# Blocks of scores turned on VectorE: all stored by one DMA and fetched by four, and a planner that counts eight transfers under way and later landings

## The chip, the cores and the metric

The kernel runs on 1 core of one Trainium2 chip. The metric is the device time of one execution in microseconds (us); the median of the runs before is 1094.97 us.

## What is computed

Two batches of 3136 tokens go through three layers, all in float32:

```python
scores = matmul(z, z.T) / S                   # z: 2 x 3136 x 64
x = u * matmul(maximum(scores, 0) ** 2, v)    # u, v: 2 x 3136 x 256
h = maximum(x @ w_in, 0)                      # 256 -> 1024
conv = sum of conv_w[k] * h shifted by k - 1  # three taps along the tokens
x = (h * sigmoid(conv)) @ w_out               # 1024 -> 256
xn = (x - mean) / sqrt(var + 1e-6) * g_ln
out = x + maximum(xn @ w_ch1, 0) @ w_ch2
```

Since the scores are z times its own transpose, the squared score block (i, j) is the transpose of block (j, i). The kernel uses that.

## The kernel before, in words

**Tiling.** A matrix product in float32 is made of three products of halves (high*high, low*high, high*low). Each batch is cut into seven chunks of queries (4, 4, 3, 4, 3, 3, 4 tiles of 128 tokens; the last tile of a batch has 64), so there are 14 chunks. For each chunk and each of the 25 tiles j of keys, a block of squared scores "a" (128 keys x 384, 448 or 512 queries) is needed. It is split into `ah` (ACT, sometimes DVE) and `al` (DVE), and six products on PE add it to the sums `av` (lines 793, 795, 796). After a chunk, `gate_u` multiplies the sums with u on DVE (line 811), and the result goes to DRAM as `gated`. The two dense layers read that back in blocks of three token tiles (`make_x`, `mlps`); their products (`hps`, `y`, `h2ps`) stand between the products of later chunks.

**Blocks that are turned instead of computed again.** A block whose mirror image was computed in an earlier chunk of the same batch is not computed. When the earlier block was made, `spill` had it turned in 32 x 32 pieces on DVE (`bl`, line 649) and stored in DRAM. `land` (lines 689 and 697) fetches it back into one of the six places of tag "a". Two ways of storing exist:

- Most blocks are stored by one DMA into `turned` (line 657) and fetched by four DMAs of 32 partitions each, in pieces of 32 elements (line 697).
- Blocks of the (chunk, later chunk) pairs in `EARLY`, here chunks 0 and 1 of the first batch for chunks 5 and 6, are stored by four DMAs in pieces of 32 elements into `mirror` (line 664) and fetched by one DMA with long rows (line 689).

In all, 154 blocks are fetched: 138 by four DMAs and 16 by one. The centred rows of the second dense layer take a similar way for most blocks of tokens (`centred<-tn` line 1064, then four DMAs `tn<-centred`, line 1070).

**What sets the order.** Nothing of the order is written by hand. `Program.order` simulates the five engines: each operation has a price per engine, a due time (worked back from the end through what depends on it, `dues`), and places in rings of buffers that it must hold. At each step an idle engine takes the operation that is ready and due first. All DMAs are issued by SP, in the planned order; an instruction of SP that waits holds up all that stand behind it. The landing of a DMA is planned from `LANDS` (1.6), its size over `RATE`, and `LATE` by name; the fetch of a block, named "land", has no `LATE`. Where the plan leaves PE idle for more than 0.225 us, products with zeros (`fill`, line 1268) are put into PE's order, one per 0.125 us of the gap. Once planned, the order of each engine is fixed, whatever the chip does.

Of the kernel before, what the change touches and what calls it, by code (L numbers as in the profile page):

```python
# [15 lines left out]
P = 128  # L16
# [7 lines left out]
SQ = 32  # L24
# [5 lines left out]
LAG0 = 130.0  # L30
LAG1 = 6.0
LAG2 = 10
EARLY = (0, 5), (0, 6), (1, 5), (1, 6)
FETCH = ("SP",)
LAND_US = {"SP": 0.56, "ACT": 0.6}

UP1, DOWN1, TURN, UP2 = 0.4, 0.14, 0.6, 0.36
LENGTH = 14.0, 14.0, 8.0, 8.0
# [36 lines left out]

AFTER = {"PE": 0.2, "ACT": 0.165, "DVE": 0.15, "POOL": 0.13, "SP": 0.0}
RATE, LANDS = 300.0, 1.6
LATE = {"z1": 1.4, "v1": 1.6, "u": 1.0, "wi": 0.8, "wo": 0.8, "w1": 0.8, "w2": 0.8, "x in": 1.2, "lh": 0.6, "spill": 0.6}
SPILL_KB, LAND_KB = 0.53, 0.91
ENGINES = ("PE", "ACT", "DVE", "POOL", "SP")  # L80

# [9 lines left out]
class Op:  # L91
    __slots__ = (
        "ways", "fn", "before", "left", "after", "bufs", "due", "ready", "start", "end", "n", "engine", "late",
        "name", "port", "kb", "adds", "spare",
    )


class Program:
# [4 lines left out]
        self.tags = tags  # L103
        self.ops, self.writers, self.readers = [], {}, {}

    def op(self, ways, fn, reads=(), writes=(), adds=(), takes=(), due=None, late=None, name="", port=False, kb=None):


        o = Op()
        o.ways, o.fn, o.due, o.late, o.name, o.port, o.kb = ways, fn, due, late, name, port, kb  # L110
        o.before, o.after, o.n = set(), [], len(self.ops)
        o.adds, o.spare = tuple(adds), None
        for k in reads:
            assert k in self.writers, (name, k)
            o.before.update(self.writers[k])
            self.readers.setdefault(k, []).append(o)
        for k in writes:
            o.before.update(self.writers.get(k, ()))
            o.before.update(self.readers.pop(k, ()))
            self.writers[k] = [o]  # L120
        for k in adds:
            o.before.update(self.readers.get(k, ()))
            self.writers.setdefault(k, []).append(o)
        o.before.discard(o)
        bufs = []
        for k in (*reads, *writes, *adds, *((t,) for t in takes)):
            if isinstance(k[0], Buf) and k[0] not in bufs:
                bufs.append(k[0])
        for b in bufs:
            b.users.append(o)  # L130
        o.bufs = bufs
        self.ops.append(o)
        return o
# [7 lines left out]
    def dues(self):  # L141
# [6 lines left out]
        for o in reversed(self.ops):  # L148
# [7 lines left out]
            for b in o.bufs:  # L156
                if b.order is not None:
                    k = b.tag, b.order
                    wanted[k] = min(wanted.get(k, o.due), o.due)

    def order(self):
        self.dues()
        for o in self.ops:
            for b in o.bufs:
                b.left = len(b.users)
            o.ready = 0.0
        live = {t: [] for t in self.tags}
        turn = {t: 1 for t in self.tags}
# [7 lines left out]
        for o in self.ops:  # L176
            if not o.left:
                enter(o)
        done, now, port, owner, moved_at = [], 0.0, 0.0, None, 0.0
        busy = dict.fromkeys(ENGINES, 0.0)  # L180
        while len(done) < len(self.ops):
            nxt = None

            def later(t):
                nonlocal nxt
                if t > now + 1e-9 and (nxt is None or t < nxt):
                    nxt = t

            def room(o):
                want = {}  # L190
                for b in o.bufs:
                    if b.taken:
                        continue
                    if b.order is not None and b.order != turn[b.tag]:
                        return False
                    want[b.tag] = want.get(b.tag, 0) + 1
                for tag, n in want.items():
                    held = [b for b in live[tag] if b.left or b.free_at > now]
                    live[tag] = held
                    if len(held) + n > self.tags[tag][0]:  # L200
                        for b in held:
                            if not b.left:
                                later(b.free_at)
                        return False
                for b in o.bufs:
                    if not b.taken and b.kind in CAPS and sum(x.kind == b.kind for x in live[b.tag]) >= CAPS[b.kind]:
                        for x in live[b.tag]:
                            if not x.left:
                                later(x.free_at)
                        return False  # L210
                return True

            moved = False
            for e in ENGINES:
                if free[e] > now + 1e-9:
                    later(free[e])
                    continue
                best = None
                for o in open_[e]:
                    if o.ready > now + 1e-9:  # L220
                        later(o.ready)
                        continue
                    if (e == "POOL" or e == "DVE" and o.port) and port > now + 1e-9 and owner != e:
                        later(port)
                        continue
                    key = (o.ways[0][0] != e, o.due, o.n)
                    if best is not None and key >= best[0]:
                        continue
                    if key[0]:

                        x = o.ways[0][0]
                        wait = max(0.0, free[x] - now) + sum(
                            p.ways[0][1] for p in open_[x]
                            if p.ways[0][0] == x and p.ready <= now and (p.due, p.n) <= (o.due, o.n)
                        )
                        if wait < HELP * dict(o.ways)[e]:
                            continue
                    if room(o):
                        best = key, o
                if best is None:  # L240
                    continue
                o = best[1]
                us = dict(o.ways)[e]
                for x, _ in o.ways:
                    open_[x].remove(o)
                o.engine, o.start, o.end = e, now, now + self.lasts(o, e, us)
                free[e] = now + us
                if o.kb is not None:
                    moved_at = max(moved_at, now + us) + o.kb / RATE
                    o.end = moved_at + LANDS + LATE.get(o.name, 0.0)  # L250
                if e == "POOL" or e == "DVE" and o.port:
                    port, owner = now + us + 0.06, e
                busy[e] += us
                later(free[e])
                for b in o.bufs:
                    if not b.taken:
                        b.taken = True
                        live[b.tag].append(b)
                        if b.order is not None:
                            turn[b.tag] += 1  # L260
                    b.left -= 1
                    b.free_at = max(b.free_at, o.end)
                for a in o.after:
                    a.left -= 1
                    a.ready = max(a.ready, o.end if a.ways[0][0] != e or e != "PE" else free[e])
                    if not a.left:
                        enter(a)
                done.append(o)
                moved = True
            if moved:  # L270
                continue
            if nxt is None:
                stuck = sorted((o for e in ENGINES for o in open_[e]), key=lambda o: o.due)
                raise RuntimeError(f"stuck at {now}: {[(o.name, o.left, [b.tag for b in o.bufs if not b.taken]) for o in stuck[:20]]}")
            now = nxt
# [26 lines left out]
def attn_moe_kernel(ctx: ExitStack, tc: tile.TileContext, zt, ut, v, w_in, conv_w, w_out, g_ln, w1, w2, out):  # L302
# [73 lines left out]
    op = pr.op  # L376
# [32 lines left out]
        return [(e, us[e]) for e in (first, *others)]  # L409

    def dma(fn, kb, **kw):
        return op([("SP", 0.45)], lambda e: fn(), late=LANDS + kb / RATE, kb=kb, **kw)


    zp = [(o, min(o + 512, ZW)) for o in range(0, ZW, 512)]
# [181 lines left out]
    centred = [dram.tile([4, SQ, NTT * D], F32, tag=f"centred{i}", name="centred") for i in range(2)]  # L597
# [30 lines left out]
    turned = {}  # L628
# [15 lines left out]
    def spill(c, j, ab):  # L644
        w = chunks[c][1] - chunks[c][0]
        b = buf("bl")
# [3 lines left out]
            reads=[(ab, 0)], writes=[(b, 0)], name="bl", port=True,  # L650
# [14 lines left out]

        if early(c, chunk_of[j]):
            op(
                [("SP", 1.95)], write_mirrored, reads=[(b, 0)], writes=[("turned", c, j)],
                late=LANDS + LAND_KB * w / RATE, kb=LAND_KB * w, due=1e4, name="spill",
            )  # L670
            return
        op(
            [("SP", 0.4)], write, reads=[(b, 0)], writes=[("turned", c, j)],
            late=LANDS + SPILL_KB * w / RATE, kb=SPILL_KB * w, due=1e4, name="spill",
        )

# [186 lines left out]
    def mlps(c):  # L863
        when = whens[c]
        s, e_ = blocks[c]
        n = e_ - s
# [186 lines left out]
        if far:  # L1053
# [14 lines left out]
            def fetch(e):  # L1068
# [4 lines left out]
                    )  # L1073

            op(
                [("SP", 2.05)], fetch, late=LANDS + n / RATE, kb=n, reads=[("centred", c % 2)], writes=[(tn, 0)],
                name="xn in",
            )

            def landed(d):  # L1080
# [261 lines left out]
```

## Time and profile before

| | us |
|---|---|
| median of 3 runs (lowest, highest) | 1094.97 (1094.73, 1096.04) |
| the profiled execution | 1097.35 |
| its span, first to last instruction | 1095.6 |
| PE busy (matmul) / PEld (weight load) | 1084.7 / 1018.4 |
| DVE / ACT / POOL busy | 881.4 / 724.2 / 37.4 |
| DMA queue of the kernel | 47.3% of 16 engines |

The times of parts below are of the profiled execution. A matmul is recorded from its start to its modelled end, and the next one starts well before that end, so the idle time of PE is less than the time that PE lost. The weight loads (PEld), one ahead of each matmul, show the lost time more directly: a load that comes late shows idle time and what ended it. The engine names are those of the profile: PE is TensorE, DVE VectorE, ACT ScalarE, POOL GpSimd, SP SyncE (SPq where it issues DMAs). The granted clock of TensorE is 1.00 throughout.

### The profile page before, as it was taken

To read this page: it belongs to the slowest core of one execution; us is meant where nothing else is said; L and a number is where in the kernel's file an instruction comes from. 1 tells how busy PE (TensorE), PEld (TensorE's weight loads), DVE (VectorE), ACT (ScalarE), POOL (GpSimd) and SP (SyncE) were. 2 spreads that over 40 slices of the span, in tenths; PEclk is the share of its full clock that TensorE was granted. 3 is DMA by queue.
4 is the path that set the end of the run, shared out by engine and by line. 5 is a ranking of instruction groups with operands and counts; after the bars stand their busy time and mean duration, and the time that the engine had idled before them with its cause. 6 is when DMAs were issued, how large, how long until landed. Compare 5 with 4: busy or idle time off the path is not lost.

```text
span 1095.6 us, 19246 instructions
## 1 busy us (share of the span) xinstructions
PE 1084.7 (99%) x6569; PEld 1018.4 (93%) x6569; DVE 881.4 (80%) x1890; ACT 724.2 (66%) x1500; POOL 37.4 (3%) x54
## 2 busy tenths in 40 slices
PE   9999999999999999999999999999999999999998
PEld 7878888999999899999999999999999999999998
DVE  7999899899996988787868788878678585868674
ACT  7768788886765767675757666656666463646452
POOL 2100000000101000000000000000000000000000
PEclk9999999999999999999999999999999999999999
DMA  6786878677867232322243425142635557520000
GB/s 203 201 202 141 191 172 184 133 201 173 231 142 166 84 101 63 102 79 79 78 115 96 110 59 129 42 111 60 156 77 121 109 99 147 96 78 25 25 16 20
DMA packets 379106, 126.45 MB, mean 115 GB/s; under 512 B 278272, under 2 KB 368896, under 8 KB 379008
## 3 DMA queue, kind: packets, MB, share of 16 engines
q1 hardware_dynamic: 379008, 125.23, 47.3%
q8 instruction: 51, 0.84, 0.3%
q14 instruction: 47, 0.39, 0.1%
HBM read 70.25 MB, written 51.97 MB: 112 GB/s over the span
## 4 chain that ended last, share of the span: by engine, by line
PE 85%; DVE 4%; DMA 4%; ACT 3%; SPq 2%; issue 1%; DVEq 0%; POOL 0%; ACTq 0%
PE av L793 11%; PE av L796 11%; PE av L795 10%; PE y L900 8%; PE y L902 8%; PE y L901 8%; PE h2ps L884 4%; PE h2ps L886 4%; PE h2ps L885 4%; PE hps L884 4%; PE hps L885 4%; PE hps L886 4%; PE s L751 3%; PE s L752 3%; DMA land<-turned 2%
## 5 line engine op out<-in xcount | busy, mean ns | idle before, releaser
L793 PE MATMUL av<-ah,vh 128*128 128x512 f32 (+2 forms) x700 | 257.4, 368 | 3.4 <-ACT ah L401 1.7
L796 PE MATMUL av<-ah,vl 128*128 128x512 f32 (+2 forms) x700 | 256.0, 366 | 0.0
L795 PE MATMUL av<-al,vh 128*128 128x384 f32 (+2 forms) x672 | 247.8, 369 | 1.8 <-DVE al L730 1.4
L793 PEld LDWEIGHTS av<-ah,vh 128*128 128x128 f32 x700 | 131.6, 188 | 16.8 <-ACT ah L401 3.3
L796 PEld LDWEIGHTS av<-ah,vl 128*128 128x128 f32 x700 | 131.5, 188 | 14.5
L795 PEld LDWEIGHTS av<-al,vh 128*128 128x128 f32 x672 | 126.2, 188 | 16.2 <-DVE al L730 6.0
L1144 ACT ACTIVATE g2h<-h2ps 128x384 fp32r<-128x384 f32 (+1 forms) x136 | 64.8, 478 | 115.8 <-PE h2ps L886 109.9
L760 ACT ACTIVATE a<-s 128x512 f32<-128x512 f32 (+2 forms) x196 | 105.9, 557 | 49.0 <-PE s L752 48.3
L1149 DVE SCALAR_TENSOR_TENSOR g2l<-h2ps,g2h 128x384 fp32r<-128x384 f32 (+1 forms) x136 | 73.0, 537 | 78.4 <-ACT g2h L1144 77.7
L730 DVE TENSOR_TENSOR al<-a,ah 128x512 fp32r<-128x512 f32 (+2 forms) x182 | 116.7, 648 | 14.1 <-ACT ah L401 13.4
L900 PE MATMUL y<-w2h,g2h 128*128 128x256 f32 x392 | 110.5, 282 | 0.6 <-DVE ysb L1159 0.4
L902 PE MATMUL y<-w2h,g2l 128*128 128x256 f32 x392 | 110.3, 281 | 0.0
L901 PE MATMUL y<-w2l,g2h 128*128 128x256 f32 x392 | 110.0, 281 | 0.0
L900 PE MATMUL y<-woh,gh 128*128 128x256 f32 x392 | 110.0, 281 | 0.0
L902 PE MATMUL y<-woh,gl 128*128 128x256 f32 x392 | 109.9, 280 | 0.0
L901 PE MATMUL y<-wol,gh 128*128 128x256 f32 x392 | 109.9, 280 | 0.0
L730 DVE TENSOR_TENSOR al<-land,ah 128x384 fp32r<-128x384 f32 (+2 forms) x154 | 92.0, 599 | 22.0 <-ACT ah L401 20.2
L769 ACT ACTIVATE a<-a 128x512 f32<-128x512 f32 (+2 forms) x183 | 105.9, 592 | 1.4
L649 DVE STREAM_TRANSPOSE bl<-a 128x512 f32<-128x512 f32 (+1 forms) x146 | 94.9, 656 | 14.8 <-ACT a L769 14.0
L401 ACT CAST ah<-a 128x512 fp32r<-128x512 f32 (+2 forms) x181 | 104.0, 582 | 3.8 <-DVE a L765 1.0
L401 ACT CAST ah<-land 128x384 fp32r<-128x384 f32 (+2 forms) x138 | 74.8, 547 | 35.0 <-DMA land<-turned 24.1
L950 ACT ACTIVATE t<-t 128x384 f32<-128x384 f32 (+1 forms) x136 | 68.7, 508 | 41.2 <-DVE t L943 40.7
(119 smaller groups left out, 2465.3 us busy)
## 6 DMA issues: line engine op xcount, KB each, us to landing
turned<-bl SPq DMA_DIRECT2D x78, 256.0 KB, 2.3
land<-turned SPq DMA_DIRECT2D x296, 48.0 KB, 2.4
turned<-bl SPq DMA_DIRECT2D x44, 192.0 KB, 2.5
land<-turned SPq DMA_DIRECT2D x120, 64.0 KB, 2.5
land<-turned SPq DMA_DIRECT2D x136, 56.0 KB, 2.4
out_dram<-ysb SPq DMA_DIRECT2D x15, 384.0 KB, 2.6
vst<-in_v_dram SPq DMA_DIRECT2D x11, 512.0 KB, 4.3
xl<-gated SPq DMA_DIRECT2D x14, 386.0 KB, 3.9
```

The lines of the kernel that those rows point to most:

```text
L401: nc.scalar.copy(dst, src)
L649: [("DVE", price("dve_turn", w))], lambda e: nc.vector.transpose(at(b, "bl")[:, :w], at(ab)[:, :w]),
L730: lambda e: nc.vector.tensor_tensor(at(al, "al")[:, :n], a(), f(at(ah)[:, :n]), ALU.subtract),
L760: [("ACT", price("act_ps", n))], lambda e: nc.scalar.activation(a(), at(ps)[:, :n], AF.Relu),
L769: op([("ACT", price("act", n))], lambda e: nc.scalar.activation(a(), a(), AF.Square), writes=[(ab, 0)], name="square")
L793: nc.tensor.matmul(p, vhj, at(ah)[:, :n], start=first(b, d), stop=False, **kw)
L795: nc.tensor.matmul(p, vhj, at(al)[:, :n], start=False, stop=False, **kw)
L796: nc.tensor.matmul(p, vlj, at(ah)[:, :n], start=False, stop=False, **kw)
L884: nc.tensor.matmul(p, a, h_, start=d == 0, stop=False)
L900: nc.tensor.matmul(p, a, wh, start=first(acc, (i0 + i) // 2), stop=False, **kw)
L901: nc.tensor.matmul(p, a, wl, start=False, stop=False, **kw)
L902: nc.tensor.matmul(p, b, wh, start=False, stop=k == NF - 1, **kw)
```

## The change

`EARLY` is empty: every turned block is stored by one DMA and fetched by four. The planner is changed in four ways. It prices the issue of DMAs by name. It has eight lanes: a DMA waits in SP's planned time until the transfer eight before it has landed. It takes other landing times by name (`MOVE` scales the bytes, `LATE` for "land" goes from nothing to 2.0 us). And it plans ten times: after each round the due times are moved by a fifth towards the latest time at which that round's operations could have started, and the best of the ten plans is kept.

```diff
-EARLY = (0, 5), (0, 6), (1, 5), (1, 6)
+EARLY = ()
 FETCH = ("SP",)
-LAND_US = {"SP": 0.56, "ACT": 0.6}
+ISSUE_US = {"lh": 0.52, "x in": 0.57, "x out": 0.57, "xn out": 0.34}
+LAND_US = {"SP": 0.47, "ACT": 0.6}
...
-LATE = {"z1": 1.4, "v1": 1.6, "u": 1.0, "wi": 0.8, "wo": 0.8, "w1": 0.8, "w2": 0.8, "x in": 1.2, "lh": 0.6, "spill": 0.6}
+ROUNDS, BLEND = 10, 0.2
+LANES = 8
+MOVE = {
+    "land": 0.83, "spill": 0.83, "wi": 1.4, "wo": 1.4, "w1": 1.4, "w2": 1.4, "u": 1.2, "x in": 1.4, "v1": 1.25, "z": 0.8,
+    "xn in": 1.4, "xn out": 0.8, "out": 0.9, "lh": 1.1,
+}
+LATE = {
+    "z1": 0.6, "v1": 0.6, "u": 0.6, "wi": 0.8, "wo": 0.8, "w1": 0.8, "w2": 0.8, "x in": 0.5, "lh": 0.9, "spill": 1.9,
+    "land": 2.0, "xn in": 2.0, "x out": 0.7, "xn out": 0.2,
+}
...
+    def latest(self, done):
+        seq, first, frees, at, last = {}, {}, {}, {}, {}
...
+        for o in reversed(done):
+            us, takes = dict(o.ways)[o.engine], o.end - o.start
+            found = [self.us - takes]
+            if o.engine in last:
+                found.append(last[o.engine] - us)
+            found += [at[a] - (us if a.engine == o.engine == "PE" else takes) for a in o.after]
+            found += [at[a] - takes for a in frees.get(o, ()) if a in at]
+            at[o] = last[o.engine] = min(found)
+        return at
+
     def order(self):
         self.dues()
+        best = None
+        for _ in range(ROUNDS):
+            done = self.once()
+            if best is None or self.us < best[0]:
+                best = self.us, self.busy, [(o, o.engine, o.start, o.end) for o in done]
+            at = self.latest(done)
+            for o in done:
+                o.due += BLEND * (at[o] - o.due)
...
+                if o.kb is not None:
+                    t = now
+                    for _ in range(o.dmas):
+                        t = max(t, lanes.pop(0)) + us / o.dmas
+                        moved_at = max(moved_at, t) + MOVE.get(o.name, 1.0) * o.kb / o.dmas / RATE
+                        lanes.append(moved_at + LANDS)
+                    us = t - now
+                    o.end = moved_at + LANDS + LATE.get(o.name, 0.0)
                 free[e] = now + us
-                if o.kb is not None:
-                    moved_at = max(moved_at, now + us) + o.kb / RATE
-                    o.end = moved_at + LANDS + LATE.get(o.name, 0.0)
...
-        return op([("SP", 0.45)], lambda e: fn(), late=LANDS + kb / RATE, kb=kb, **kw)
+        return op([("SP", ISSUE_US.get(kw["name"], 0.42))], lambda e: fn(), late=LANDS + kb / RATE, kb=kb, **kw)
```

Counted over the whole program, 52 DMAs `mirror<-bl` and 16 `land<-mirror` go; 14 `turned<-bl` and 64 `land<-turned` come, ten DMAs more in all. PE has the same 6462 products of the work and 105 with zeros instead of 107. POOL has 11 instructions fewer, DVE 6 and ACT 5 more. The rest of the change is order. Lines of the changed kernel stand 53 further down there (`land` line 697 is line 750).

**SP, ahead of the first fetched block of the kernel** (`lh` is an operand of chunk 1's scores; `land` the first fetched block of chunk 1). Before:

```order
L664 DMA mirror<-bl 32x16x32 x4
L590 DMA lh<-hl 64x384
L591 DMA lh<-hl 64x384
L664 DMA mirror<-bl 32x16x32 x16
L697 DMA land<-turned 32x16x32 x4
L817 DMA gated<-u 256x1x512
```

Changed:

```order
L710 DMA turned<-bl 128x4x128
L643 DMA lh<-hl 64x384
L644 DMA lh<-hl 64x384
L710 DMA turned<-bl 128x4x128
L750 DMA land<-turned 32x16x32 x4
L870 DMA gated<-u 256x1x512
```

Sixteen DMAs ahead of the four of the fetch have become one.

**SP, from the operands `lh` of chunk 6 on, where chunk 5's blocks are fetched.** Before (the twelve rows from that `lh` on):

```order
L590 DMA lh<-hl 64x448
L689 DMA land<-mirror 128x384
L591 DMA lh<-hl 64x448
L657 DMA turned<-bl 128x3x128 x2
L689 DMA land<-mirror 128x384
L831 DMA xl<-gated 128x2x386
L657 DMA turned<-bl 64x3x128
L689 DMA land<-mirror 128x384
L817 DMA gated<-u 256x1x384
L689 DMA land<-mirror 128x384 x3
L604 DMA u<-in_ut_dram 128x2x384
L697 DMA land<-turned 32x12x32 x16
```

Changed:

```order
L643 DMA lh<-hl 64x448
L644 DMA lh<-hl 64x448
L750 DMA land<-turned 32x12x32 x44
L870 DMA gated<-u 256x1x384
L750 DMA land<-turned 32x12x32 x16
L750 DMA land<-turned 32x14x32 x4
L657 DMA u<-in_ut_dram 128x2x384
L750 DMA land<-turned 32x14x32 x12
L611 DMA wst<-in_w_dram 128x2x512 x2
```

Single fetches between other DMAs have become 76 DMAs for 19 blocks, with two others among them. PE's products from the first use of the first of these 19 blocks to the first use of the last are 206 in the changed order: 156 of 384 or 386 columns, 20 of 448 and 30 of 256.

**PE, within chunk 1: products with zeros.** Before:

```order
L751 MATMUL s<-hl 128x512
L752 MATMUL s<-lh,hl 128x512
L1268 MATMUL warm_ps<-zero 128x256 x9
L793 MATMUL av<-ah,vh 128x512
L795 MATMUL av<-al,vh 128x512
L796 MATMUL av<-ah,vl 128x512
L793 MATMUL av<-ah,vh 128x512
L795 MATMUL av<-al,vh 128x512
L796 MATMUL av<-ah,vl 128x512
L751 MATMUL s<-hl 128x512
L752 MATMUL s<-lh,hl 128x512
L1268 MATMUL warm_ps<-zero 128x256 x7
```

Changed, after the same six `s` products and at about the same count of products:

```order
L804 MATMUL s<-hl 128x512
L805 MATMUL s<-lh,hl 128x512
L937 MATMUL hps<-xh,wih 128x386
L938 MATMUL hps<-xl,wih 128x386
L939 MATMUL hps<-xh,wil 128x386
L937 MATMUL hps<-xh,wih 128x386
L938 MATMUL hps<-xl,wih 128x386
L939 MATMUL hps<-xh,wil 128x386
L846 MATMUL av<-ah,vh 128x512
```

The sixteen products with zeros are gone from chunk 1, and products of the first dense layer stand there earlier. Towards the end of chunk 0 and at its border to chunk 1 the changed order has 25 where before had 9. DVE has 97 instructions ahead of the first `gate_u`, before 91.

## Rows read from the trace of the kernel before

**Rows 1.** The page's busy time: engine, us, share, instructions, of the whole span
```profile
PE 1084.7 (99%) x6569; PEld 1018.4 (93%) x6569; DVE 881.4 (80%) x1890; ACT 724.2 (66%) x1500; POOL 37.4 (3%) x54
```
**Rows 2.** Waits of the weight loads, whole span: us in total, times, longest
```profile
PEld av L795 <- DVE al L730: 6.0, 15, 0.7
PEld av L793 <- ACT ah L401: 3.3, 5, 1.3
```
**Rows 3.** The same, of 0 to 110 us
```profile
PEld av L795 <- DVE al L730: 2.9, 6, 0.7
```
**Rows 4.** The same, of 110 to 150 us
```profile
PEld av L793 <- ACT ah L401: 1.5, 2, 1.3
PEld av L795 <- DVE al L730: 1.4, 4, 0.4
```
**Rows 5.** The same, of 250 to 300 us
```profile
PEld av L795 <- DVE al L730: 0.8, 2, 0.4
```
**Rows 6.** The same, of 360 to 960 us
```profile
PEld y L900 <- DVE ysb L1159: 1.4, 4, 0.4
```
**Rows 7.** Timeline of SP from 54 us: start, us, DMAs issued
```profile
54.65 9.44 SPq L664 DMA_DIRECT2D mirror<-bl  x16
64.19 2.06 SPq L697 DMA_DIRECT2D land<-turned  x4
```
**Rows 8.** The chain that ended last: start, us, what (products with zeros)
```profile
79.25 1.08 PE warm_ps L1268 x9
82.25 0.84 PE warm_ps L1268 x7
```
**Rows 9.** Timeline of PEld from 67.5 us; in brackets the idle time before it
```profile
69.19 0.19 PEld L793 LDWEIGHTS av<-ah,vh 128*128 128x128 f32 x1 [1.10 <-ACT ah L401]
69.92 0.19 PEld L795 LDWEIGHTS av<-al,vh 128*128 128x128 f32 x1 [0.54 <-DVE al L730]
```
**Rows 10.** Timeline of SP from 127 us
```profile
127.17 0.50 SPq L558 DMA_DIRECT2D wst<-in_w_out_dram  x1
127.76 2.00 SPq L697 DMA_DIRECT2D land<-turned  x4
```
**Rows 11.** Timeline of ACT at 134 us
```profile
133.92 0.51 ACT L401 CAST ah<-land 128x384 fp32r<-128x384 f32 x1 [3.53 <-DMA land<-turned]
```
**Rows 12.** Line 697, fetches in four: issue in ns, and us to landing
```profile
L697 SPq DMA_DIRECT2D land<-turned x552: 302/469/2610, 64.2 to 964.1; - x184
...
DMA to landing us min/median/max: 1.9/2.4/6.2
```
**Rows 13.** Line 689, fetches in one: the same
```profile
L689 SPq DMA_DIRECT2D land<-mirror x16: 319/504/902, 240.0 to 289.4; - x16
...
DMA to landing us min/median/max: 2.9/4.4/6.0
```
**Rows 14.** Timeline of SP from 194 us: two long runs of fetches
```profile
194.91 10.47 SPq L697 DMA_DIRECT2D land<-turned  x20
...
209.11 10.20 SPq L697 DMA_DIRECT2D land<-turned  x20
```
**Rows 15.** Windows: stretch, busy us of PE, PEld, DVE, ACT, POOL, clock, DMA, GB/s
```profile
0.00:110.00 110.00, 107.05 (x480) 87.11 (x481) 98.61 (x175) 83.26 (x160) 12.13 (x23) 1.00 0.72 187
...
200.00:205.00 5.00, 4.94 (x25) 4.24 (x24) 4.83 (x13) 4.96 (x13) 0.00 (x0) 1.00 0.61 97
...
245.00:250.00 5.00, 4.85 (x30) 4.60 (x28) 4.25 (x10) 3.35 (x8) 0.00 (x0) 1.00 1.03 322
```
**Rows 16.** Timeline of PE from 352 us: two lengths of product
```profile
352.52 0.34 PE L885 MATMUL h2ps<-xtl,w1h 128*128 128x384 f32 x1
352.70 0.34 PE L886 MATMUL h2ps<-xth,w1l 128*128 128x384 f32 x1
352.87 0.36 PE L793 MATMUL av<-ah,vh 128*128 128x448 f32 x1
353.07 0.37 PE L795 MATMUL av<-al,vh 128*128 128x448 f32 x1
```

More of the change, by code (lines that the diff above doesn't have):

```diff
@@ L93 @@
         "ways", "fn", "before", "left", "after", "bufs", "due", "ready", "start", "end", "n", "engine", "late",
-        "name", "port", "kb", "adds", "spare",
+        "name", "port", "kb", "adds", "spare", "dmas",
     )
@@ L104, in __init__, with op @@
         self.ops, self.writers, self.readers = [], {}, {}
-    def op(self, ways, fn, reads=(), writes=(), adds=(), takes=(), due=None, late=None, name="", port=False, kb=None):
+    def op(self, ways, fn, reads=(), writes=(), adds=(), takes=(), due=None, late=None, name="", port=False, kb=None, dmas=1):
         o = Op()
@@ L111, in op @@
         o.before, o.after, o.n = set(), [], len(self.ops)
-        o.adds, o.spare = tuple(adds), None
+        o.adds, o.spare, o.dmas = tuple(adds), None, dmas
         for k in reads:
@@ L159, in dues, with once @@
                     wanted[k] = min(wanted.get(k, o.due), o.due)
+    def latest(self, done):
+        seq, first, frees, at, last = {}, {}, {}, {}, {}
+        for o in done:
+            for b in o.bufs:
+                if b not in first:
+                    first[b] = o
+                    seq.setdefault(b.tag, []).append(b)
+        for tag, bufs in seq.items():
+            for b, x in zip(bufs, bufs[self.tags[tag][0] :]):
+                for u in b.users:
+                    frees.setdefault(u, []).append(first[x])
+        for o in reversed(done):
[7 more added lines that the diff above has]
+        return at
     def order(self):
         self.dues()
+        best = None
[4 more added lines that the diff above has]
+            at = self.latest(done)
+            for o in done:
+                o.due += BLEND * (at[o] - o.due)
+        self.us, self.busy, done = best
+        for o, *got in done:
+            o.engine, o.start, o.end = got
+        return [o for o, *_ in done]
+    def once(self):
         for o in self.ops:
+            o.left = len(o.before)
             for b in o.bufs:
-                b.left = len(b.users)
+                b.left, b.taken, b.free_at = len(b.users), False, 0.0
             o.ready = 0.0
@@ L179, in order @@
         done, now, port, owner, moved_at = [], 0.0, 0.0, None, 0.0
+        lanes = [0.0] * LANES
         busy = dict.fromkeys(ENGINES, 0.0)
@@ L667, in spill @@
             op(
-                [("SP", 1.95)], write_mirrored, reads=[(b, 0)], writes=[("turned", c, j)],
-                late=LANDS + LAND_KB * w / RATE, kb=LAND_KB * w, due=1e4, name="spill",
+                [("SP", 1.9)], write_mirrored, reads=[(b, 0)], writes=[("turned", c, j)],
+                late=LANDS + LAND_KB * w / RATE, kb=LAND_KB * w, dmas=P // SQ, due=1e4, name="spill",
             )
@@ L672, in spill @@
         op(
-            [("SP", 0.4)], write, reads=[(b, 0)], writes=[("turned", c, j)],
+            [("SP", 0.38)], write, reads=[(b, 0)], writes=[("turned", c, j)],
             late=LANDS + SPILL_KB * w / RATE, kb=SPILL_KB * w, due=1e4, name="spill",
@@ L1075, in mlps @@
             op(
-                [("SP", 2.05)], fetch, late=LANDS + n / RATE, kb=n, reads=[("centred", c % 2)], writes=[(tn, 0)],
-                name="xn in",
+                [("SP", 1.7)], fetch, late=LANDS + n / RATE, kb=n, reads=[("centred", c % 2)], writes=[(tn, 0)],
+                name="xn in", dmas=P // SQ,
             )
```

## The prediction, made before the changed kernel ran

> **What bounds the kernel now.** Read first the busy times of the page [rows 1]: PE is busy for 99% of the span, so only lost PE time can be won, or work of PE taken away. Matmuls overlap in the record, so read next who made the weight loads wait [rows 2]. All lines of that view add up to 17.4 us, 1.2 of them at the start, which nothing here touches. The two largest are `al`, the low half of a block (6.0 us, 15 times), and `ah`, the high half (3.3 us, 5 times). Then cut the same view by time: 6.0 us of the waits lie before 110 us (the 1.2 of the start among them), 3.8 from 110 to 150, 2.2 from 150 to 300, 1.2 to 360, 3.4 to 960 and 0.6 after; the largest of the stretches are in [rows 3 to 6]. To these come 107 products with zeros. Nine of them took 1.08 us [rows 8], 0.12 each, 12.8 us in all; some of them fill time in which PE would have waited anyway.
>
> So at most some 16 us of waits and a part of 12.8 us can be won. Last, see why the waits come: the timelines of SP show what a fetch stood behind [rows 7, 10], and ACT shows how long a block was late [rows 11].
>
> All numbers come from one execution, with a span of 1095.6 us and a time of 1097.35 us, 2.4 above the median of 1094.97. I work out differences and apply them to the median.
>
> **The change part by part.**
>
> *Products with zeros.* 105 instead of 107: 2 x 0.12 = 0.24 us less. More of it is a move. The sixteen in chunk 1 stood on the chain that ended last (1.08 + 0.84 = 1.92 us [rows 8]), so they cost their whole time, and they go. Sixteen come at the end of chunk 0. There DVE is nearly full: 98.61 us of 110 busy with 175 instructions, 0.56 each [rows 15]. The changed order gives it six instructions more before the first `gate_u`, 6 x 0.56 = 3.4 us, while PE gets some 1.1 us more of real products there. If DVE alone sets that border, PE loses 3.4 - 1.1 = 2.3 us, under which the new zeros are hidden; if not, nothing is lost but their own 1.9. Sum: -0.24 - 1.92 + (0 to 2.3), so -2.2 to +0.2. I take -0.2, near the upper end, because DVE is that full.
>
> *Mirror stores.* Sixteen issues occupied SP for 9.44 us ahead of the kernel's first fetch [rows 7], and PE then waited 1.10 us for its `ah` and 0.54 for its `al` [rows 9]. In the changed order one store stands there. Gain 1.6 at most, nothing at least, if DVE makes the same products late anyway. I take -1.3, near the upper end, since the wait for `ah`, ACT's part, came first and was the longer one.
>
> *Later planned landings, 110 to 150 us.* The plan of before gives a fetched block the landing time of an undisturbed one. The chip's median is 2.4 us from issue, the longest 6.2 [rows 12]. The worst case of the stretch: a weight load is issued just ahead of a fetch [rows 10], and ACT then waits 3.53 us for the block [rows 11]; in the stretch PE's loads wait 1.5 us for `ah` and 1.4 for `al` [rows 4], of 3.8 in all. The new plan puts landings 2.0 us later, and its order has that fetch ahead of the weight load. Ends: all 3.8 gone, or none. The waits for `ah` and the `al` behind it go first; I take -2.3.
>
> *Four fetches in place of one, in chunks 5 and 6.* One fetch took SP about 0.5 us [rows 13]; in long runs four take 4 x 10.47/20 = 2.1 or 4 x 10.20/20 = 2.04 [rows 14]. Sixteen blocks thus cost SP 16 x 1.55 = 25 us more. SP is off the path unless its queue runs dry of lead. The place where it could is the new run of 76 fetches with two other DMAs: 78 x 0.51 = 39.8 us. PE's products from the first use to the last take, from start to start, 0.175 us for 384 columns, 0.20 for 448 [rows 16] and 0.12 for 256 [rows 8]: 156 x 0.175 + 20 x 0.20 + 30 x 0.12 = 34.9. So SP falls back by 4.9 us over the run. The last block needs 2.4 us to land, 0.5 for `ah` [rows 11] and about as much for `al`, so the first must have been begun 4.9 + 3.4 = 8.3 us before its use. The six places of the ring allow about six times 34.9/18 = 1.9 us, 11.6, less what the places that hold blocks computed on the spot shorten. It fits, barely. What goes: the waits from 250 to 300 us, 1.3 us in all, 0.8 of them for `al` [rows 5]. Ends: -1.3 if all is hidden, +4.0 if the ring opens one place late, twice 1.9 and a little. I take +0.8, nearer to the middle, since 20 fetches in a row stood twice before [rows 14] without such waits, but 76 never.
>
> The Trainium skill (DMA: Bandwidth & Descriptors, section Issuing engines are not separate DMA queues) says that the time that issuing takes on the sequencer is usually small beside the transfer. The trace differs here: 0.51 us of issue against 2.4 to landing, four times per block, one after the other. By that rule this term would be -1.3 and the result 1089.4, which is the third rival below.
>
> The stores improve and the fetches worsen in piece length. While SP fetched in pieces of 32 elements and little else moved, 0.61 of the DMA engines' time gave 97 GB/s; with long rows 1.03 gave 322 [rows 15]. So fetches in a row alone take some 0.6, and other loads beside them lengthen landings; that is in the +4.0.
>
> *The rest* (150 to 250 and 300 to 960 us: 5.5 us of waits). Much of it waits for `ysb` [rows 6] and `u` on DVE, which longer planned landings touch only through the order. Each stretch may lose its waits or get others: -3 to +2, I take -0.5. POOL's eleven instructions fewer and ACT's five more lie under PE's work: ACT has 371 us of idle time. The stretch after 960 us has the same order but for the place of two zeros: nothing.
>
> Sum: -0.2 - 1.3 - 2.3 + 0.8 - 0.5 = -3.5, so 1094.97 - 3.5 = **1091.5 us**.
>
> **The rivals.**
>
> *DVE, not the landing, is late.* `al` makes PE wait more often than `ah` (15 times against 5 [rows 2]), and DVE has six instructions more. If the earlier landings only make blocks wait for DVE, the second and third terms shrink from -3.6 to about -1 and the result is some 1094, no change. Against it: the long idle time of ACT before the late block [rows 11], in which DVE's part could not begin.
>
> *SP becomes the bound* (the other side). Should the ring let SP begin the run with 6 us of lead instead of 8.3, each block from the middle of the run on comes late, and PE is held at SP's pace: +4.0 in place of +0.8. The lead is decided by how early DVE splits the block six places before. With half of the second and third terms (-1.8) and the others as above (-0.7) that gives +1.5; with other fetches delayed as well, up to +3: 1096.5 to 1098. For it: 39.8 us of issue against 34.9 of products. Against it: the planner itself prices SP at 0.47 per fetch and spaced PE's work by that.
>
> *The run of fetches costs nothing.* If SP's lead suffices and what waited from 250 to 300 us goes with the fetches in one, that term is -1.3 in place of +0.8: the sum is -5.6, the result 1089.4. For it: two runs of 20 fetches [rows 14] without a wait of PE that a landing ended. Against it: 4.9 us of lead lost in one run.
>
> *More is won.* If the wider landing times and ten rounds also take most of the 5.5 us of the rest and the fillers turn out hidden: -0.2 becomes -2.2, -0.5 becomes -3, and the sum -8: 1087.
>
> *That the change does not do what it says* is excluded by the order: no DMA to or from `mirror` is left, and the four fetches are there.
>
> **How the numbers follow.** A measurement of this kernel can tell 0.2%, 2.2 us, from no change, so faster is below 1092.8 and slower above 1097.2. Forecast (1090 to 1094.5): 0.38, most of it below 1092.8. Run of fetches hidden: 0.12. DVE late: 0.22, no change. SP the bound: 0.18, slower. More won: 0.10. From these: faster 0.54 (0.32 of the forecast, 0.12 and 0.10 of the two that win more), no change 0.28 (0.22 and the forecast's other 0.06), slower 0.18. The forecast's own range is 1090 to 1094.5. The range that holds the time 8 times in 10 reaches from just under the case of more won, 1086, to the upper end of the rival of SP, 1098.
>
> **What would show it.** Right: the waits of weight loads for `ah` and `al` between 60 and 150 us fall from some 5 us (1.6 in [rows 9], 2.9 in [rows 4]) to 2; no wait of 1 us there behind a fetch; the zeros in chunk 1 gone without new idle time of PE in that place; SP issuing without a pause for 40 us near 255 to 295 us, with ACT waiting for landings there by no more than 2 us in all. Wrong: waits for `ah` behind landings that grow along that run (then SP is the bound), or the same total of waits with `al` in the first place and ACT no longer waiting for landings (then DVE is), or new waits of PE in places that the old plan served well, which would say that the order of ten rounds is no better on the chip.

## The result and the profile after

The changed kernel takes **1110.74 us** (median; 1108.35 to 1111.46), the kernel before 1095.22 beside it: ratio 1.013, 95% interval 1.0115 to 1.0144. The medians differ by 15.5 us, slower, where I forecast 3.5 us less; the ratio of 1.013 stands for 14.2 us, and below I go by ratios. The profiled execution took 1111.46 us with a span of 1109.2; that of before had 1095.6.

The busy time of PE says little [rows 1]; the page of after:

```profile
PE 1086.5 (98%) x6567; PEld 1018.2 (92%) x6567; DVE 880.0 (79%) x1896; ACT 728.5 (66%) x1505; POOL 29.7 (3%) x43
```

PE, DVE and ACT work about as long as before, and the span is 13.6 us longer. All waits of the weight loads add up to 30.0 us, before to 17.4. The same, cut by time as in [rows 3 to 6], says where. After, 110 to 150 us (before: 3.8 us in all [rows 4]):

```profile
PEld av L846 <- DVE u L864: 0.2, 1, 0.2
```

After, 235 to 345 us, all lines of the view:

```profile
PEld av L848 <- DVE al L783: 4.0, 11, 0.4
PEld y L955 <- DVE gl L1019: 4.0, 4, 2.7
PEld av L846 <- DVE ah L789: 2.6, 1, 2.6
PEld av L846 <- ACT ah L454: 2.1, 5, 1.0
PEld y L953 <- ACT gh L454: 2.0, 2, 1.2
PEld av L846 <- issue: 1.9, 1, 1.9
PEld y L954 <- DVE w2l L595: 0.3, 1, 0.3
```

That is 16.9 us, where before had 1.6 in the same stretch. So 3.6 us were won at 110 to 150 us and some 15 lost in chunks 4 to 6. Seven different lines in one stretch speak for one cause behind the engines that they name. The same stretch by windows, first before, then after (columns as in [rows 15]):

```profile
235.00:345.00 110.00, 109.59 (x663) 105.76 (x662) 99.85 (x215) 77.24 (x162) 5.41 (x6) 1.00 0.74 180
```

```profile
235.00:345.00 110.00, 99.47 (x567) 90.81 (x565) 81.16 (x174) 63.27 (x133) 1.49 (x2) 1.00 0.68 142
```

PE, DVE, ACT and the DMA engines are all less busy after than before: 99.85 to 81.16 us on DVE, 0.74 to 0.68 for DMA. What remains to look at is SP. Its timeline after, with the 16 fetches ahead of the run of 76 and that run (start, us, DMAs issued; two issues of `lh` stand between the first two rows):

```profile
240.31 11.53 SPq L750 DMA_DIRECT2D land<-turned  x16
253.17 24.31 SPq L750 DMA_DIRECT2D land<-turned  x44
277.52 0.57 SPq L870 DMA_DIRECT2D gated<-u  x1
278.19 10.52 SPq L750 DMA_DIRECT2D land<-turned  x20
288.76 0.48 SPq L657 DMA_DIRECT2D u<-in_ut_dram  x1
289.34 6.14 SPq L750 DMA_DIRECT2D land<-turned  x12
```

SP issues without a pause for 42.3 us, from 253.17 to 295.48, while PE has 34.9 us of products for these 19 blocks: 7.4 us too little. PE went at SP's pace: from the first use of the first block at 257.70 to the first use of the last at 300.00, 206 products took it 42.3 us as well. All waits of its loads from 250 to 300 us are 3.4 (`al`) + 2.1 (`ah`) + 1.9 = 7.4 us. The 1.9 us under "issue" are SP's too: `gate_u` (line 864), ahead of that load, waited for the DMA of `u` that SP issued at 288.76, behind 64 fetches (timelines of DVE, PEld and PE after, idle time in brackets):

```profile
292.57 0.56 DVE L864 SCALAR_TENSOR_TENSOR u<-av,u 128x384 f32<-128x384 f32 x1 [2.66 <-DMA u<-in_ut_dram]
294.24 0.19 PEld L846 LDWEIGHTS av<-ah,vh 128*128 128x128 f32 x1 [1.87 <-issue]
300.00 0.37 PE L846 MATMUL av<-ah,vh 128*128 128x448 f32 x1
```

ACT, whose cast follows the landing, waits block by block (timeline of ACT, idle time in brackets):

```profile
270.05 0.52 ACT L454 CAST ah<-land 128x384 fp32r<-128x384 f32 x1 [0.99 <-DMA land<-turned]
272.24 0.51 ACT L454 CAST ah<-land 128x384 fp32r<-128x384 f32 x1 [1.25 <-DMA land<-turned]
275.25 0.51 ACT L454 CAST ah<-land 128x384 fp32r<-128x384 f32 x1 [1.46 <-DMA land<-turned]
277.29 0.52 ACT L454 CAST ah<-land 128x384 fp32r<-128x384 f32 x1 [1.14 <-DMA land<-turned]
```

One block in 2.0 to 3.0 us is SP's pace for four fetches. The landings themselves are no longer than before [rows 12]; line 750 after:

```profile
DMA to landing us min/median/max: 1.8/2.4/6.3
```

### The profile page after: what moved, and what is told of

It reads as the page before. It is cut to its first block, busy times and chain, and to the rows that moved or that the text cites. A ratio compares the mean times of both kernels' runs of the same rounds, so it can differ in the third digit from the quotient of the medians.

```text
span 1109.2 us, 19268 instructions
## 1 busy us (share of the span) xinstructions
PE 1086.5 (98%) x6567; PEld 1018.2 (92%) x6567; DVE 880.0 (79%) x1896; ACT 728.5 (66%) x1505; POOL 29.7 (3%) x43
## 4 chain that ended last, share of the span: by engine, by line
PE 82%; DMA 6%; DVE 4%; SPq 4%; ACT 1%; issue 1%; POOL 0%; DVEq 0%; ACTq 0%
PE av L846 10%; PE av L849 10%; PE av L848 10%; PE y L953 8%; PE y L955 8%; PE y L954 7%; SPq L750 4%; PE hps L938 4%; PE hps L937 4%; PE hps L939 4%; PE h2ps L937 4%; PE h2ps L939 4%; PE h2ps L938 4%; PE s L804 3%; PE s L805 3%; DMA land<-turned 2%
## 5 line engine op out<-in xcount | busy, mean ns | idle before, releaser
L454 ACT CAST ah<-land 128x384 fp32r<-128x384 f32 (+2 forms) x142 | 77.5, 548 | 54.1 <-DMA land<-turned 48.9
L454 ACT CAST ah<-a 128x512 fp32r<-128x512 f32 (+2 forms) x176 | 101.2, 587 | 2.7 <-PE av L849 0.7
L988 DVE SCALAR_TENSOR_TENSOR t<-h,cw,t 128x384 f32<-128x384 f32 (+1 forms) x136 | 80.6, 597 | 22.6 <-ACT t L979 22.1
```

Of the source, the lines that this page charges most:

```text
L454: nc.scalar.copy(dst, src)
```

## The experiments

Theory 1: SP has not the time to issue four fetches per block in chunks 5 and 6. Theory 2: the new planner's order is worse on the chip, however blocks are fetched. Each kernel ran beside runs of the kernel before, whose medians lay between 1094.5 and 1095.9 us; I compare by ratio.

**e1 to e4: planner and fetches apart.** e1 is the changed kernel, e2 the kernel before, each with the other's `EARLY` (the diff is that of e1; e2 is the reverse):

```diff
-EARLY = ()
+EARLY = (0, 5), (0, 6), (1, 5), (1, 6)
```

e3 and e4 hold the order of PE, ACT, DVE and POOL row for row and change the DMAs alone. In e3 (the changed order) the 16 blocks are stored by four DMAs (`write_mirrored`) and the first of the four planned fetches fetches all, the other three issue nothing. In e4 (the order before) `write` stores by one DMA, and the planned single fetch issues four.

> The changed kernel with EARLY as before (16 blocks stored by four DMAs and fetched by one), planned anew by the new planner. Theory 1 (SP's issue of the fetches is the bound of chunks 5 and 6): most of the 15 us comes back, 1091 to 1098 us, and the waits of weight loads between 235 and 345 us fall from 17 us to under 5. Theory 2 (the order of the new planner is worse on the chip, however the blocks are fetched): 1104 to 1111 us.

> The kernel before with EARLY empty, nothing else, planned anew by the old planner. Theory 1: slower than before by 8 to 20 us (1103 to 1115), with the new waits in chunks 5 and 6. Theory 2: as before, 1093 to 1098 us.

> The order of the changed kernel on PE, ACT, DVE and POOL, row for row, but the 16 blocks are stored by four DMAs each and fetched by one, in the places of the plan's one and four. Only SP's queue differs. Theory 1: the waits of weight loads between 235 and 345 us fall to under 6 us; the stores cost up to 2 us more in the first 110 us; 1094 to 1101 us. Theory 2: 1106 to 1111 us.

> The order of the kernel before on PE, ACT, DVE and POOL, row for row, but the 16 blocks are stored by one DMA and fetched by four. Theory 1: SP needs 16 x 1.55 = 25 us more in chunks 5 and 6, in places where the plan left it no room: 1102 to 1116 us. Theory 2: 1093 to 1097 us.

| | one fetch | four fetches |
|---|---|---|
| old planner | before: 1 | e2: 1106.47 us, 1.010 (1.0077 to 1.0123) |
| new planner | e1: 1097.74 us, 1.002 (1.001 to 1.0031) | after: 1.013 (1.0115 to 1.0144) |
| old order, row for row | before: 1 | e4: 1114.51 us, 1.0176 (1.0157 to 1.0194) |
| new order, row for row | e3: 1101.70 us, 1.0058 (1.0037 to 1.008) | after: 1.013 |

e1, e2 and e4 fell in the range of theory 1, e3 just above it (1101.7 against 1101; its waits from 235 to 345 us are 6.2 us, where I had said under 6). With four fetches each planner is slow, with one neither is by much: 8 to 19 us go with the fetches. Theory 2 keeps 0.2% (e1) to 0.6% (e3, which also has the stores by four).

e4 holds more than SP's time. In parts of it the granted clock of TensorE was the lower of its two levels, 1.2 in place of 2.4 GHz. PE's loads had been held just before or were held then: for 1.7 us up to 246.3 and 2.2 us up to 249.9, for 2.0 us up to 264.4, and for 6.3 us up to 312. The window of e4, where the changed kernel kept a mean clock of 1.00:

```profile
235.00:345.00 110.00, 96.25 (x534) 89.91 (x533) 82.06 (x176) 62.29 (x130) 3.62 (x4) 0.92 0.70 147
```

The mean clock there is 0.92, so at most 8% of 110 us, 8.8 us of PE's work, went with the clock (an estimate).

e2's plan shows the same shortage from the inside. The old planner prices a fetch at 0.56 us and sees that SP is short, so it leaves gaps for PE and fills them: e2's program has 176 products with zeros, the kernel before 107. In the trace of e2, those products alone, by windows (us and count of PE, PEld and DVE):

```profile
235.00:345.00 110.00, 9.20 (x65) 8.77 (x65) 0.00 (x0) 0.98 0.71 151
```

The changed kernel has none from 110 to 345 us; there the same shortage stands in the trace as waits.

**e5: the price.** The new planner prices a fetch at 0.47 us, the length of one issue in the record. From start to start it is 0.51 and more [rows 14].

```diff
-LAND_US = {"SP": 0.47, "ACT": 0.6}
+LAND_US = {"SP": 0.52, "ACT": 0.6}
```

> The changed kernel with the plan's price of one fetch DMA at 0.52 us (measured start to start: 0.51 to 0.55) instead of 0.47, planned anew. Theory 1 (SP has not the time for four fetches per block in chunks 5 and 6, whatever the plan knows): still slow, 1102 to 1110 us; what the chip waited for now stands in the plan as products with zeros, some 49 of which the new order has in the second half of batch one and later. Theory 3 (the plan only mispriced the fetch; told the price it finds a good order): 1094 to 1100 us.

1103.04 us, ratio 1.007 (1.0052 to 1.0088): in the range of theory 1, near its lower end. The plan now sees the shortage (145 products with zeros, 45 of them between 150 and 345 us) and orders around a part of it: some 7 us of the loss came back. The rest did not.

**e6, e7: stores by four at another time.** The pairs in `EARLY` are moved to chunks whose blocks are stored after 110 us, in the new planner (e6, the diff) and the old (e7, the same from the four pairs of before):

```diff
-EARLY = ()
+EARLY = (2, 5), (2, 6), (3, 5), (3, 6)
```

> The changed kernel with EARLY = (2,5), (2,6), (3,5), (3,6): the 14 blocks fetched by one DMA are those that are stored after 110 us, not in the first 110 us. Theory 4 (storing by four DMAs costs some 5 us where it stands in the first 110 us, because it holds up SP there; fetching by four costs 15 us in chunks 5 and 6): both are avoided, 1089 to 1095 us, faster than before. If stores by four cost the same wherever they stand: 1095 to 1099 us.

> The kernel before with the same later pairs in EARLY. Theory 4: 1088 to 1094 us. If stores by four cost the same wherever they stand: 1094 to 1098 us.

1101.66 us, 1.0066 (1.0047 to 1.0085), and 1103.47 us, 1.0071 (1.0056 to 1.0086). Theory 4 fell, and neither expectation held: both are worse than before and than stores that cost the same everywhere would make them. The stores moved into a stretch in which SP has less room: in e7 they stand between 131 and 266 us, and before between 47 and 120. In e7 the waits there are those for fetched blocks (weight loads, 110 to 345 us):

```profile
PEld av L795 <- DVE al L730: 6.4, 15, 1.0
PEld av L793 <- ACT ah L401: 4.3, 5, 2.1
```

In the kernel before, SP issued 27 and 22 DMAs in the two stretches of 20 us from 60 us on, and 36 and 31 in the two from 200 us on; a full stretch holds some 38 (an estimate, 20 us over 0.52). In e7 the five stretches from 140 us on have 31 to 36 each, where before the first three have 25 to 28. The old pairs had put the additional DMAs where SP had room, and saved them where it had less. That this is the whole of e6's and e7's loss is argued, not shown.

**e8 to e11: another issuer.** `FETCH` is a list of the planner's choices; a fetch that SP can't issue soon may go to ACT:

```diff
-FETCH = ("SP",)
+FETCH = ("SP", "ACT")
```

e8 is this in the changed kernel, e9 in the kernel before, e10 in the kernel before with `EARLY` empty, e11 in e5.

> The changed kernel with fetches issued by SP or, where SP is busy, by ACT (107 of 616 by ACT), planned anew. Theory 1 (the issue on SP is the bound, not the short pieces on the DMA engines): much of the 15 us comes back, 1096 to 1105 us. If the DMA engines with their short pieces are the bound: 1107 to 1113 us.

> The kernel before with fetches issued by SP or, where SP is busy, by ACT (120 by ACT). If SP's issue also costs the kernel before some of its waits at 110 to 150 us: 1089 to 1094 us; if the issues only take time from ACT: 1096 to 1100 us.

> The kernel before with EARLY empty and fetches by SP or ACT (139 by ACT). Theory 1: the stores by one give back their 5 us in the first 150 us, and the fetches by four no longer wait for SP: 1088 to 1096 us, against 1106.5 with SP alone. If the old plan has other reasons to be slow without EARLY: over 1101 us.

> The changed kernel with the price of 0.52 us for a fetch on SP and fetches by SP or ACT (128 by ACT). Theory 1: price and relief together, 1091 to 1097 us, no slower than with the price of 0.47 (1097.1). If the price matters only where SP is full: the same as with 0.47.

e8: 1097.14 us, 1.0017 (1.0006 to 1.0028), with 128 fetches by ACT in its trace (the expectation says 107). The bytes and the pieces are those of the changed kernel, the DMA engines are busier (0.80 from 235 to 345 us, against 0.68), and the loss is nearly gone:

```profile
235.00:345.00 110.00, 106.31 (x632) 100.89 (x630) 96.04 (x210) 70.65 (x150) 5.66 (x6) 1.00 0.80 169
```

So SP's issuing is the bound, not the short pieces on the DMA engines. ACT's fetches also run in a DMA queue of their own (q10, beside SP's q1), so e8, which is also planned anew, does not tell SP's time for the instructions from a backlog in SP's queue. e9: 1099.70 us, 1.0035 (1.0023 to 1.0047): where SP has room, issues by ACT only cost, by the second of its expectations. e10: 1102.68 us, 1.0065 (1.0047 to 1.0084), 3.8 us better than e2, but in the range of its second expectation (over 1101): the old plan without `EARLY` is slow for other reasons too, and which these are stays open. e11: 1099.39 us, 1.0036 (1.0021 to 1.0051), no better than e8, as its second expectation had it: the price matters only where SP is full.

**e12: the price with room on SP.** e1 with 0.52 in place of 0.47.

> The changed kernel with EARLY as before and the price of 0.52 us. With the price of 0.47 it took 1097.7. If the new plan's remaining 1.8 us over the kernel before come from the price: 1093 to 1096 us. If they come from its other parts (landing times, lanes, ten rounds): 1097 to 1101 us.

1100.39 us, 1.0039 (1.0024 to 1.0054), so the price is not what e1 has over before. It also shows the grain of such comparisons: each new price or pair makes a new plan, and plans without a shortage differ by some 3 us. The runs that hold the order row for row are free of that.

**s1, s2: stores by one without fetches by four.** In both, the 16 blocks are stored by one DMA and fetched by one with long rows from the same bytes, so that the turning across the 32 x 32 pieces is left out and what they compute is not the result; the order is held row for row (s1 of before, s2 of the changed kernel).

```diff
-                        in_=mirror[src, c % per][r0 : r0 + P, :n]
+                        in_=turned[src][j - start_of[i]][g0 * SQ : g0 * SQ + n, :]
+                        .rearrange("r x -> (r x)").rearrange("(p y) -> p y", p=P)
```

> The order of the kernel before on PE, ACT, DVE and POOL, row for row; the 16 blocks are stored by one DMA and fetched by one with long rows, so that they arrive with their 32 x 32 pieces in the wrong places (the turning across pieces is left out). Only the stores differ from before, 14 DMAs in place of 52. If the waits at 110 to 150 us came from the stores by four holding up SP: those waits fall from 3.7 to under 1 us, 1089 to 1093 us. If they came from landings that the plan put too early, as I predicted: the waits stay, 1094 to 1097 us.

> The order of the changed kernel, row for row, stored by one and fetched by one in the same way (the turning across pieces left out), so that against the changed kernel only the fetches of 16 blocks differ. The price of these fetches by four in the new order: if SP's issue is nearly all of the loss, 1095 to 1099 us; if the new order is bad for other reasons too, 1100 to 1106.

s1: 1093.57 us, 0.9983 (0.9975 to 0.9992). The waits from 110 to 150 us are gone, with the old plan and its early landings; the whole view of s1 there:

```profile
PEld av L793 <- DVE u L811: 0.4, 1, 0.4
```

e1 has the new plan with its later landings and stores by four, and keeps them:

```profile
PEld av L846 <- ACT ah L454: 1.8, 3, 0.9
PEld av L848 <- DVE al L783: 1.6, 4, 0.4
```

So the gain at 110 to 150 us is that of the stores: fewer DMAs of SP ahead of the fetches. Of the 3.4 us of waits, 1.9 arrive in the time of s1. In the new order the same step, e3 against s2, is 0.58% - 0.15% = 0.43%, 4.7 us; what the stores are worth depends on the order that they stand in.

s2: 1096.41 us, 1.0015 (1.0006 to 1.0024). Against the changed kernel only the fetches of 16 blocks differ: 1.3% - 0.15% = 1.15%, 12.6 us. In the old order the same step (e4 against s1) is 1.76% + 0.17% = 1.93%, 21 us, of which up to 8.8 are e4's lower clock. The waits of s2 from 235 to 345 us, all lines:

```profile
PEld av L851 <- DVE ah L794: 2.5, 1, 2.5
PEld av L851 <- ACT ah L455: 1.1, 2, 0.8
PEld av L853 <- DVE al L788: 1.0, 3, 0.4
```

The 2.5 us in one piece are in the changed kernel as well (2.6), so they do not come from the 16 blocks' fetches. ACT stands behind its cast of a block's `xl` until that has landed (timeline of ACT after; in s2 it waits 1.94 us there):

```profile
242.29 0.51 ACT L454 CAST xh<-xl 128x386 fp32r<-128x386 f32 x1 [1.98 <-DMA xl<-gated]
```

**v1, v3, v2: half of the relief.** `EARLY` is (0,5), (1,5) in v1 (old planner) and v2 (new planner), and (1,5), (1,6) in v3 (old planner).

> The kernel before with EARLY = (0,5), (1,5): only chunk 5's blocks, where fetches stand closest, are fetched by one; half of the stores by four go. If SP's shortage is in chunk 5 alone: 1090 to 1095 us, faster than both kernels; if chunk 6 needs the relief as well: 1097 to 1103.

> The kernel before with EARLY = (1,5), (1,6): half of the blocks fetched by one in both chunks. If half of the relief is enough: 1090 to 1095 us; if not: 1097 to 1102.

> The changed kernel with EARLY = (0,5), (1,5). With the old planner these pairs took 1095.9 us, no slower than all four pairs. If half of the relief is enough for the new plan too: 1093 to 1098 us; if its tighter runs of fetches need all of it: 1099 to 1105 us.

v1: 1095.89 us, 1.0008 (0.9999 to 1.0017), between its expectations: the same as before. The head gains what chunks 5 and 6 lose: the waits of the weight loads up to 150 us fall from 9.8 to 4.8 us, those from 235 to 345 rise from 1.6 to 5.2. v3: 1097.40, 1.002 (1.0011 to 1.003), in its second range. v2: 1103.98, 1.0086 (1.0064 to 1.0109), in its second range too: the new plan needs the whole relief. No kernel that computes the whole beats the kernel before.

**w1: later landings alone.** e1 without `"land": 2.0` in `LATE`.

> The new planner with EARLY as before (run e1, 1097.7 us) without the 2.0 us that it adds to the landing of a fetched block; all else as in e1. If later planned landings are worth what I predicted (2.3 us at 110 to 150 us, more elsewhere): 1100 to 1106 us, with more waits for ah behind landings. If they are worth nothing once SP has room: 1095 to 1099 us.

1106.32 us, 1.0108 (1.0083 to 1.0133), 0.9% slower than e1 and at the upper end of its first expectation. ACT's waits for fetched blocks, over the whole span, in e1 and then in w1:

```profile
ACT ah L454 <- DMA land<-turned: 26.2, 21, 3.1
```

```profile
ACT ah L454 <- DMA land<-turned: 47.3, 40, 3.1
ACT ah L454 <- DMA land<-mirror: 5.7, 5, 1.8
```

So the 2.0 us are worth some 9 us to the new plan, which is more than the 3 us by which plans differ. They do not make it better than the old one, which had 24.1 and 3.6 us of these waits without them.

## Why the prediction was wrong

**The step that failed** is the fourth term, four fetches in place of one: "It fits, barely", +0.8 us. It measured 12.6 us (after against s2). Its first half was right: I had 39.8 us of issue against 34.9 us of products, and the run took 42.3. The second half took the ring of six places for what sets the lead, 11.6 us against 8.3 needed. The first block of the run shows the lead that there was: its first fetch is issued at 253.17 and PE's loads for it are held until 257.69 and 258.29 (timeline of PEld after):

```profile
257.69 0.19 PEld L846 LDWEIGHTS av<-ah,vh 128*128 128x128 f32 x1 [0.20 <-ACT ah L454]
258.29 0.19 PEld L848 LDWEIGHTS av<-al,vh 128*128 128x128 f32 x1 [0.41 <-DVE al L783]
```

That is 4.5 us, no more than three issues of 0.55, the median landing of 2.4 and the cast of 0.5. The ring did not hold SP up in the run. Where a place is still taken, SP pauses ahead of a fetch until DVE has split the block in it, as ahead of 131.85 us (waits of SP after, 128 to 133 us):

```profile
SPq L750 <- DVE al L783: 1.8, 1, 1.8
```

From 209 to 332 us SP never paused for longer than 0.33 us between two instructions. The ring offered places, but SP could not use them: it was issuing all the time. The 16 fetches from 240.31 on took it 0.72 us each, because one of them took 2.7 us and one 1.4; what held these two is open. So the whole deficit went to PE, and went on into the stretch up to 345 us. There `gh` and `gl` of the dense layer stood on ACT and DVE behind late casts of blocks and of a part of `z`, whose load SP had issued at 331.09 (timeline of ACT after):

```profile
329.68 0.56 ACT L454 CAST ah<-land 128x448 fp32r<-128x448 f32 x1 [1.77 <-DMA land<-turned]
330.15 0.51 ACT L454 CAST gh<-t 128x384 fp32r<-128x384 f32 x1
335.24 0.62 ACT L454 CAST hl<-zst 128x512 fp32r<-128x512 f32 x1 [3.78 <-DMA zst<-in_zt_dram]
```

With the 16 blocks fetched by one (s2) no load waits for `gh` or `gl` there. I should have carried the sum of SP over the whole stretch in which it is full, not over one run with an assumed lead at its start. The upper end of +4.0 ("one place late") was of the same mould and too small. The argument against the rival, that the planner "spaced PE's work by that", rested on the very price that was 0.04 us per fetch too low, by the pace in [rows 14], and 0.08 by that of the run of 44.

**Right, or right in sign.** The rival of SP named the mechanism, place and sign; it put the term at +4.0, a third of its price, and the whole at 1.5 to 3 us slower. That ACT would wait block by block along the run was the sign I gave for it. By the rule of the Trainium skill (DMA: Bandwidth & Descriptors, section Issuing engines are not separate DMA queues) the sequencer's time for issuing is usually small beside the transfer. The runs don't agree here: 128 fetches moved from SP to ACT, with the same bytes and pieces, brought 1097.1 us in place of 1110.7 (e8).

**Right size, wrong cause.** The waits at 110 to 150 us fell by 3.6 us, where the third term had -2.3. But s1 and e1 show that the stores by one do this and later landings don't. The second term (stores, -1.3) put the stores' gain before 110 us alone; there the waits went from 6.0 to 7.0 us: the 1.1 us for `ah` went, those for `al` stayed at 2.9, those for ACT's `a` rose from 0.4 to 2.1, and 0.8 came under "issue".

**The first term** (zeros, -0.2): before 110 us the zeros take 12.9 us in both kernels, and the waits rose by 1.0 us; by these sums the moved zeros cost what they saved. **The rest** (-0.5): from 150 to 235 us the waits are 1.2 us against 0.6 and after 360 us 4.3 against 4.0, nothing.

Put together by the row-for-row runs: stores -1.9 us (s1), the new order +3.5 (s2 against s1), four fetches +12.6 (after against s2): 14.2 us, the ratio of 1.013, to which these three add up by the way that they are taken. Taken by e3, the new order is +6.4, the stores -4.7 (s2 against e3) and the fetches the same. What of the new order's 3.5 us comes from which part of the planner is open; 2.5 of it is the one wait behind `xl`.

## What to carry to other kernels

An engine that only issues DMAs has a capacity too: count its instructions per stretch at their start-to-start time, and before splitting a transfer into four, look whether the queue has room at that place, not on average. Additional DMAs belong where the issuer idles, even if that makes another transfer worse there. A price taken from the record of one instruction leaves out the gap to the next; a planner that is told 0.47 for 0.52 us believes in room that does not exist.

## What the runs showed of the chip that I had not expected

The issue of a fetch is recorded as 0.47 us (median), but a run of 44 took 24.31 us, 0.55 each, and runs of 20 took 0.51 to 0.53. The 0.55 is no steady pace: most issues of that run start 0.51 us apart, and single ones take longer, up to 1.55 us. With the DMA engines at 0.64 to 0.68 of their time and landings unchanged at a median of 2.4 us, the issuing on SP alone slowed the whole core by 1%.
